# Linear attention and a cosine FFN in one planned program: copies of reciprocals on another engine, fewer weight tiles on GpSimd, other due dates

## Chip, cores and metric

One core of a Trainium2 chip runs the whole program. Its engines each take their own instructions strictly in order: TensorE (PE, with PEld for the weight load ahead of a matmul), VectorE (DVE), ScalarE (ACT), GpSimd (POOL) and SyncE (SP), which here only issues DMAs. The metric is device time in microseconds (us), the median over the runs of a kernel; lower is better.

## What is computed

Attention with an exponential feature map, without a softmax over keys, and behind it a feed-forward layer with the activation h cos(h). Sizes: batch 8, 8 heads, 576 positions, head width 64, 128 features; 4608 tokens, model width 512, inner width 2048, all in fp32.

```python
def phi(x):
    proj = np.einsum('bhsd,df->bhsf', x, w_phi)
    proj = proj - np.max(np.abs(proj), axis=-1, keepdims=True)
    return np.concatenate([np.exp(proj), np.exp(-proj)], axis=-1)
q_p, k_p = (phi(q), phi(k))
kv = np.einsum('bhsf,bhsd->bhfd', k_p, v)
z = np.sum(k_p, axis=2)
num = np.einsum('bhsf,bhfd->bhsd', q_p, kv)
den = np.einsum('bhsf,bhf->bhs', q_p, z)[..., None] + 1e-06
x = (num / den).transpose(0, 2, 1, 3).reshape(B * S, H * D)
h = x @ w_in
out = (h * np.cos(h)) @ w_out
```

## The kernel before, in words

**Attention.** The work is cut into 32 units, u0 to u31; a unit is two heads of one batch, so four units make a batch. Each unit runs one chain of steps: `load` and `load_v` (SP); `q_mm` (PE, L383), `q_copy` out of PSUM (ACT, L390), `q_red`, `q_max` and `q_turn` (DVE, L394, L402 and L404, L408), which bring the largest magnitude of each query position to all partitions; `q_sub` (POOL, L412); `k_mm` (PE, L437 and L440) and `k_max` (DVE, L447 and L449); `exp_k` and `exp_q` (ACT, L456 and L461); `kv_mm` (PE, L496 and L502) and `kv_out` (ACT, L510 and L511); `z_mm` (PE, L527) for the denominators, `invert` (DVE, L540 to L543) for their reciprocals; `spread` (POOL, L550), which copies the 9 reciprocals of each of 32 partitions to where the next step wants them, eight copies of 32x9 a unit; `turn` (DVE, L554), `n_mm` (PE, L535) for the numerators, `times` (DVE, L558), and `store`.

**FFN.** Tokens are cut into 9 chunks of 512, c0 to c8, and the inner width into 16 weight tiles, f0 to f15. A chunk and a weight tile give one FFN tile, 144 in all: `mm1` (PE, 12 matmuls, L641), `copy` out of PSUM (ACT, L647 and L648), `reduce` of the angle (DVE, L652), `cosine` (ACT, L656), `times` (DVE, L659), `high` (ACT, L48) and `low` (DVE, L53), `mm2` (PE, 12 matmuls, L675 to L677), which adds into four PSUM banks. Each operand is split into a high and a low part, so each product takes three matmuls. Before its first use each weight tile is unpacked and split (`convert`): `scale` and `high` on ACT, `bits` on DVE (L307, L309, L311), and three operations of 128x1024, `rest`, `low`, `add` (L318, L53, L324), on POOL for f0 to f7 and on DVE for f8 to f15.

**Stages.** Units u0 to u15 run at the start, together with the conversion of the weight tiles and the first visits of c0, c1 and c2; then FFN tiles of c0 to c2 run alone; then units u16 to u31 run beside c3 to c5, one unit to about three FFN tiles; at the end c6 to c8 run alone.

**Order.** Nothing is scheduled while the kernel runs. Every step is a `Step` with an engine, a cost, what it depends on, the buffers of a ring that it takes, and a due time. `plan()` (L81) walks forward in its own time: of the steps of an engine that could start within 0.05 us of the earliest, it takes the one with the least due time. On ACT a step that needs another function table counts as due 8 us later. A step with `port=True` also waits for, and holds, one shared resource: the SBUF way that DVE and POOL share. PSUM has 8 banks, and past the due time `FFN_DUE` attention steps may hold at most `A_BANKS` of them. The result is one fixed instruction order per engine.

ACT has to load a function table (ACT_TABLE_LOAD) when it goes from exponentials to the sine of `cosine` or back.

Of the kernel before, what the change touches and what calls it, by code (L numbers as in the profile page):

```python
# [17 lines left out]
P = 128  # L18
# [7 lines left out]
def phi_attention_then_cos_ffn(ctx: ExitStack, tc: tile.TileContext, qT, kT, vS, vT, w_phi, w_in, w_out, out):  # L26
# [40 lines left out]
    class Step:  # L67
        def __init__(self, eng, cost, fn, deps=(), take=(), use=(), due=0.0, lat=None, table=None, port=False):
            self.eng, self.cost, self.fn, self.due, self.table = eng, cost, fn, due, table
            self.deps = [d for d in deps if d is not None]  # L70
            self.take, self.use = list(take), list(use)
            self.port = port
            self.lat = LATENCY[eng] if lat is None else lat
            self.start = None
            for b in self.take + self.use:
                b.users.append(self)
            steps.append(self)

    LATENCY = dict(PE=0.35, ACT=0.25, DVE=0.2, POOL=0.25, SP=2.2)

    def plan():  # L81
# [15 lines left out]
        table = None  # L97
# [129 lines left out]
    A_BANKS = 5  # L227
    FFN_DUE = 60.0
    W_POOL = range(8)
# [24 lines left out]
    for v, (c, fts) in enumerate(course):  # L254
# [3 lines left out]
        for ft in fts:  # L258
            if ft not in seen:
                seen.add(ft)  # L260
                date_w[ft] = advance(0, W_DVE)[0]
            date_tile[n] = advance(T_PE, T_DVE)
            n += 1
            if v > 8 and len(date_unit) < NU and n % 3 == 0:
                date_unit[len(date_unit)] = advance(U_PE, U_DVE)
        at["DVE"] = max(at["DVE"], at["PE"] - 15)

    def due_unit(u, f):

        return date_unit[u][0] + f * max(date_unit[u][1], 20.0) - (0 if u < NBT else 16.0)  # L270
# [12 lines left out]
    def convert(ft):  # L283

        d = {}
        due = date_w[ft] - 14.0
# [56 lines left out]
    def reload(ft, after, due):  # L343
# [6 lines left out]
        w_ready[ft] = [Step("SP", 3.2, load, w_stored[ft] + [after], take=[slot], due=due)]  # L350
# [5 lines left out]
    stored, quotient = {}, {}  # L356

    def attention(u):
        d = {}
        early = u < EARLY  # L360
        due = lambda f: due_unit(u, f)
# [13 lines left out]
        ld = Step("SP", 1.9, load, take=[b["kr"], b["qr"]], due=due(-1.5))  # L375
        lv = Step("SP", 0.9, load_v, take=[b["v"]], due=due(-0.9))
# [33 lines left out]
        def q_sub(j):  # L410
            c = slice(j * S, (j + 1) * S)
            POOL.tensor_tensor(out=d["pq"][:, c], in0=d["pq"][:, c], in1=d["bq"][:, c], op=ALU.subtract)  # L412

        reds, mm = [], None
        for hf in range(2):
# [3 lines left out]
                      use=[b["qr"]] + ([b["pq"]] if hf else []), due=due(0.0))  # L419
            for j in range(2):  # L420
                cp = Step("ACT", 0.31, lambda hf=hf, j=j: q_copy(hf, j), [mm] + reds[:1], use=[pair[j], b["pq"]],
                          due=due(0.05))
                reds.append(cp)
        cps, reds = reds, []
        for i, cp in enumerate(cps):
            reds.append(Step("DVE", 0.42, lambda i=i: q_red(i // 2, i % 2), [cp], use=[b["pq"]], due=due(0.1)))
        qm = Step("DVE", 0.94, q_max, reds, take=[b["bq"]], use=[b["pq"]], due=due(0.15))
        qm = Step("DVE", 1.4, q_turn, [qm], use=[b["bq"]], due=due(0.16))
        qs = [Step("POOL", 1.5, lambda j=j: q_sub(j), [qm], use=[b["pq"], b["bq"]], due=due(0.2), port=True) for j in range(2)]


# [32 lines left out]
        for i in range(3):  # L464
            ps = d["kb", i] = Buf("bank", "a")
            pk = Buf("pk" if i < 2 else "pk_t")
            mm = Step("PE", 0.9 if i < 2 else 0.35, lambda i=i: k_mm(i), [ld], take=[ps, pk], use=[b["kr"]], due=due(0.12))
            kms.append(Step("DVE", 1.3 if i < 2 else 0.55, lambda i=i: k_max(i), [mm], use=[ps, pk], due=due(0.2)))
# [46 lines left out]
        for i in range(3):  # L515
            last = Step("PE", 1.15 if i < 2 else 0.5, lambda i=i: kv_mm(i), [lv, last] + (eks[i:i + 1] if early else eks),
                        take=[] if i else [acc, b["kv"]], use=[ekb[i], b["v"]] + ([acc, b["kv"]] if i else []), due=due(0.55))
        ko = Step("ACT", 0.6, kv_out, [last], use=[acc, b["kv"]], due=due(0.6))
# [19 lines left out]
        def invert():  # L538
# [4 lines left out]
            DVE.reciprocal(out=dn, in_=dn)  # L543

        def spread():
            d["d1"] = new("rb", [P, 2 * NJ], F32, f"d1_u{u}_", "d1")
            for g in range(4):
                for a in range(2):
                    r = 64 * (g // 2) + 32 * a
                    POOL.tensor_copy(out=d["d1"][r:r + 32, (g % 2) * NJ:(g % 2 + 1) * NJ], in_=d["dn"][32 * g:32 * g + 32])  # L550
# [14 lines left out]
        mm = Step("PE", 1.1, z_mm, [ko] + eqs, take=[zps], use=[b["kv"]] + eqb, due=due(0.72))  # L565
        dv = Step("DVE", 0.85, invert, [mm], take=[b["rb"]], use=[zps], due=due(0.8))
        dv = Step("POOL", 1.9, spread, [dv], use=[b["rb"]], due=due(0.8), port=True)
        dv = Step("DVE", 0.78, turn, [dv], use=[b["rb"]], due=due(0.81))
        outs = []
        for hf in range(2):  # L570
            ps = d["nb", hf] = Buf("bank", "a")
            mm = Step("PE", 1.05, lambda hf=hf: n_mm(hf), [mm], take=[ps], use=[b["kv"]] + eqb, due=due(0.75))
            outs.append(Step("DVE", 0.45, lambda hf=hf: times(hf), [mm, dv], use=[ps, b["rb"]], due=due(0.82)))
        stored[u] = Step("SP", 0.9, store, outs, use=[b["rb"]], due=due(0.9))
# [11 lines left out]
    def visit(v):  # L586
        c, fts = course[v]
        d = {}
        n0 = sum(len(x[1]) for x in course[:v])
# [5 lines left out]
        for kt in range(KT):  # L595
# [12 lines left out]
            chain["x"] = [Step("SP", 0.9, load, [stored[NHP * bt + kt] for bt in batches] + chain["x"], take=[raw], due=due_tile(n0, -2))]  # L608
            loads += chain["x"]
        for kt in range(KT):  # L610
# [11 lines left out]
            h = Step("ACT", 0.53, high, loads[kt] if v == 0 else [loads[kt]], take=[x], use=[rawb[kt]], due=due_tile(n0, -1))  # L622
            ks.append(Step("DVE", 0.68, low, [h], use=[x, rawb[kt]], due=due_tile(n0, -1), port=True))
# [4 lines left out]
        for i, ft in enumerate(fts):  # L628
# [53 lines left out]
            s1 = Step("PE", 2.75, mm1, ks + w_ready[ft] + chain["mm1"], take=[ps, hs], use=xb + [slot], due=due_tile(n, 0.0))  # L682
            chain["mm1"] = [s1]
            s2 = Step("ACT", 1.18, copy, [s1], take=[g], use=[ps, hs], due=due_tile(n, 0.3))
            s3 = Step("DVE", 0.74, reduce, [s2], use=[g, hs], due=due_tile(n, 0.4), port=True)
            s4 = Step("ACT", 0.62, cosine, [s3], use=[g], due=due_tile(n, 0.6), table="s")
            s5 = Step("DVE", 0.66, times, [s4], use=[g, hs], due=due_tile(n, 0.8), port=True)
# [93 lines left out]
```

## Time and profile before

| what | value |
|---|---|
| median of 3 runs | 1213.09 us (1210.26 to 1213.25) |
| the profiled execution | 1212.26 us |
| its span, first to last instruction | 1210.5 us |
| instructions | 19112 |
| mean granted TensorE clock | 0.98 |
| POOL busy | 225.5 us, 358 instructions |
| DMA | 160.77 MB, mean 133 GB/s |

The span is the window in which the profile sees instructions; the 1.8 us beside it are start and end of the execution. Busy times of an engine are sums over its instructions. Names such as `pq_u__7912` are tiles: `u` stands for a unit, `c` for a chunk, `f` for a weight tile, and the number tells one buffer from another. `bank` is PSUM.

### The profile page before, as it was taken

The page shows a single profiled execution, that of the slowest core. Times are in us where ns is not written, and L with a number is a line of the kernel's source. Part 1 is how long each engine was busy: PE and PEld are TensorE (multiplying, and loading weights), DVE is VectorE, ACT ScalarE, POOL GpSimd, SP SyncE. Part 2 cuts the span into 40 slices and gives each one's busy share as a digit, 9 for nine tenths or more (in the row PEclk, how much of TensorE's full clock was granted, in tenths as well). Part 3 has the DMA queues.
Part 4 walks back from the last instruction along what each step waited for, and adds up shares of the span by engine and source line. Part 5 has one row for each costly group of instructions (what it writes and reads, how often), then busy time and mean ns, then how long its engine had stood idle before and what let it go on. Part 6 is the DMA issues. An engine that isn't in the chain of part 4 may idle for free.

```text
span 1210.5 us, 19112 instructions
## 1 busy us (share of the span) xinstructions
PE 1142.1 (94%) x7360; PEld 849.1 (70%) x7360; DVE 774.7 (64%) x1310; ACT 700.3 (58%) x1262; POOL 225.5 (19%) x358
## 2 busy tenths in 40 slices
PE   7776989899999999999998999999999999999997
PEld 5544646568668888767675766677677788888886
DVE  6999797997879755456666565675555534433432
ACT  6555758678666554556556555584666645544442
POOL 2556554620110000011111111121111100000000
PEclk9988989999999999999998999999999999999999
DMA  5444552743664523354212542236510360250350
GB/s 172 141 166 145 188 186 104 226 136 122 232 186 174 191 87 108 127 204 140 86 50 84 184 145 98 59 102 216 174 29 11 132 221 23 105 179 30 120 193 36
DMA packets 92764, 160.77 MB, mean 133 GB/s; under 512 B 43776, under 2 KB 52224, under 8 KB 84480
## 3 DMA queue, kind: packets, MB, share of 16 engines
q1 hardware_dynamic: 92672, 159.54, 39.5%
q8 instruction: 58, 0.95, 0.3%
q14 instruction: 34, 0.28, 0.1%
HBM read 117.57 MB, written 41.94 MB: 132 GB/s over the span
## 4 chain that ended last, share of the span: by engine, by line
PE 69%; ACT 11%; DVE 6%; DMA 3%; issue 1%; POOL 0%; SPq 0%; DVEq 0%; ACTq 0%
PE bank L641 27%; PE bank L675 10%; PE bank L676 9%; PE bank L677 9%; PE bank L535 3%; PE bank L437 3%; PE bank L496 3%; PE bank L527 2%; PE bank L383 1%; ACT L456 1%; ACT L656 1%; PE bank L502 1%; PE bank L440 0%; DVE m_u__1467 L404 0%; DVE o L717 0%
## 5 line engine op out<-in xcount | busy, mean ns | idle before, releaser
L656 ACT ACT_TABLE_LOAD x24 | 30.8, 1283 | 0.4
L550 POOL COPY d_u__4884<-dn_u__4879 32x9 f32<-32x9 f32 x8 | 2.2, 275 | 150.8 <-DVE dn_u__4879 L543 150.5
L456 ACT ACT_TABLE_LOAD x21 | 26.9, 1283 | 2.3 <-DVE pk_u__6191 L449 2.0
L717 DVE COPY o<-bank 128x512 f32<-128x512 f32 x18 | 12.1, 682 | 13.5 <-PE bank L677 10.5
L715 ACT ACTIVATE o<-bank 128x512 f32<-128x512 f32 x18 | 10.6, 597 | 12.9 <-PE bank L677 10.7
L711 DVE TENSOR_TENSOR o<-bank,o 128x512 f32<-128x512 f32 x24 | 15.5, 682 | 0.3
L641 PE MATMUL bank<-xh_c__5003,w 128*128 128x512 f32 x32 | 13.7, 429 | 0.0
L641 PE MATMUL bank<-xh_c__4449,w 128*128 128x512 f32 x32 | 13.5, 421 | 0.0
L641 PE MATMUL bank<-xh_c__6056,w 128*128 128x512 f32 x32 | 13.4, 418 | 0.0
L641 PE MATMUL bank<-xh_c__7275,w 128*128 128x512 f32 x32 | 12.7, 396 | 0.0
L641 PE MATMUL bank<-xh_c__5512,w 128*128 128x512 f32 x32 | 12.6, 393 | 0.0
L641 PE MATMUL bank<-xh_c__4491,w 128*128 128x512 f32 x32 | 12.6, 393 | 0.0
L641 PE MATMUL bank<-xh_c__6530,w 128*128 128x512 f32 x32 | 12.6, 393 | 0.0
L641 PE MATMUL bank<-xh_c__5325,w 128*128 128x512 f32 x32 | 12.5, 392 | 0.0
L641 PE MATMUL bank<-xh_c__4454,w 128*128 128x512 f32 x32 | 12.5, 392 | 0.0
L641 PE MATMUL bank<-xh_c__5774,w 128*128 128x512 f32 x32 | 12.5, 392 | 0.0
L641 PE MATMUL bank<-xh_c__6341,w 128*128 128x512 f32 x32 | 12.5, 391 | 0.0
L641 PE MATMUL bank<-xh_c__4537,w 128*128 128x512 f32 x32 | 12.5, 391 | 0.0
L641 PE MATMUL bank<-xh_c__6802,w 128*128 128x512 f32 x32 | 12.5, 391 | 0.0
L641 PE MATMUL bank<-xh_c__7477,w 128*128 128x512 f32 x32 | 12.5, 390 | 0.0
L641 PE MATMUL bank<-xh_c__7820,w 128*128 128x512 f32 x32 | 12.5, 390 | 0.0
L641 PE MATMUL bank<-xh_c__7674,w 128*128 128x512 f32 x32 | 12.5, 390 | 0.0
(3810 smaller groups left out, 4250.0 us busy)
## 6 DMA issues: line engine op xcount, KB each, us to landing
w<-w_parts SPq DMA_DIRECT2D x48, 1024.0 KB, 4.8
w_parts<-w SPq DMA_DIRECT2D x16, 1024.0 KB, 4.8
out<-o SPq DMA_DIRECT2D x36, 256.0 KB, 2.1
vmain<-vS SPq DMA_DIRECT2D x32, 256.0 KB, 3.9
sums<-o SPq DMA_DIRECT2D x24, 256.0 KB, 2.2
o<-sums SPq DMA_DIRECT2D x24, 256.0 KB, 3.0
vtail<-vT SPq DMA_DIRECT2D x64, 16.0 KB, 2.8
w_raw_f__139<-w_in SPq DMA_DIRECT2D x1, 512.0 KB, 4.2
```

The source lines that it names most:

```text
L383: PE.matmul(out=ps[j], lhsT=wphi[r, :], rhs=d["qr"][r, hf * HALF:(hf + 1) * HALF], start=True, stop=True)
L437: PE.matmul(out=ps[:, 256 * x:256 * x + 256], lhsT=d["kr"][:, P * s:P * s + P], rhs=wk_f, start=(x == 0), stop=True, skip_group_check=True)
L456: ACT.activation(out=e[:, :, s * P:(s + 1) * P], in_=pk, func=AF.Exp, scale=1.0 - 2.0 * s)
L496: PE.matmul(out=acc[c:c + 64, n, j, :], lhsT=e[:, 2 * x + j, P * n + c:P * n + c + 64], rhs=vmain[u % 2][:, s, j, :], start=(s == 0 and j ...
L527: PE.matmul(out=ps[32 * g:32 * g + 32], lhsT=d["z"][:, 2 * n + j, :], rhs=d["eq", j][:, n, hf * HALF:(hf + 1) * HALF], start=(n == 0), sto ...
L535: PE.matmul(out=ps[64 * j:64 * j + 64], lhsT=d["kv"][:, 2 * n + j, :], rhs=d["eq", j][:, n, t], start=(n == 0), stop=(n == 1))
L641: PE.matmul(out=h, lhsT=a[:, cs], rhs=d[b, kt], start=(k == 0), stop=(k == 3 * KT - 1))
L656: ACT.activation(out=m["g"], in_=m["g"], func=AF.Sin, bias=halfpi, scale=1.0)
L675: PE.matmul(out=a, lhsT=gh[:, t], rhs=w[:, 0], start=first, stop=False)
L676: PE.matmul(out=a, lhsT=gh[:, t], rhs=w[:, 1], start=False, stop=False)
L677: PE.matmul(out=a, lhsT=gl[:, t], rhs=w[:, 0], start=False, stop=last)
L711: DVE.tensor_tensor(out=o, in0=bank(acc[tb]), in1=o, op=ALU.add)
```

## The change

Five things change; what is computed stays.

1. `invert` writes the reciprocals straight into the wider tile `d1`, in both of its halves (128x18 instead of 128x9), and `spread` is four ACT copies of 32x9, each between partition groups that are neighbours, instead of eight POOL copies.
2. POOL takes `rest`, `low` and `add` of f0 to f3 alone; those of f4 to f7 go to DVE.
3. The planner counts `q_max` and `invert` as users of the way that DVE and POOL share, too, and charges 0.1 us when PE goes between FFN and attention matmuls.
4. `A_BANKS` is 6 instead of 5, and the `load_v` of a unit comes behind that of the unit before.
5. Every kind of step has a shift of its due time (`EARLIER`, in us, by kind and stage). The names `SPAN`, `SHIFT`, `EVERY`, `LEAD`, `TURN` and `SLACK` hold the values that stood in the code before.

```diff
-        def __init__(self, eng, cost, fn, deps=(), take=(), use=(), due=0.0, lat=None, table=None, port=False):
-            self.eng, self.cost, self.fn, self.due, self.table = eng, cost, fn, due, table
+        def __init__(self, eng, cost, fn, deps=(), take=(), use=(), due=0.0, lat=None, table=None, port=False, kind=""):
+            self.eng, self.cost, self.fn, self.table = eng, cost, fn, table
...
+            self.kind, self.due = kind, due + EARLIER.get(kind, 0.0)
...
+            if eng == "PE":
+                self.table = "x" if fn.__name__ in ("mm1", "mm2", "one") else "f"
...
+    EARLIER = {
+        "a.exp_k": 3, "a.exp_q": 17, "a.invert": -86, "a.k_mm": 27, "a.kv_mm": 3, "a.kv_out": 40, "a.load": 4,
...
-            if x.eng == "ACT" and x.table is not None and x.table != table:
-                c += 1.3
-                table = x.table
+            if x.table not in (None, table.get(x.eng)):
+                c += 1.3 if x.eng == "ACT" else 0.1
+                table[x.eng] = x.table
...
-    A_BANKS = 5
+    A_BANKS = 6
...
-    W_POOL = range(8)
+    W_POOL = range(4)
...
-        lv = Step("SP", 0.9, load_v, take=[b["v"]], due=due(-0.9))
+        lv = Step("SP", 0.9, load_v, [chain_v.get(u - 1)], take=[b["v"]], due=due(-0.9), kind=phase + "load_v")
...
-        qm = Step("DVE", 0.94, q_max, reds, take=[b["bq"]], use=[b["pq"]], due=due(0.15))
+        qm = Step("DVE", 0.94, q_max, reds, take=[b["bq"]], use=[b["pq"]], due=due(0.15), port=True, kind=phase + "q_max")
...
-            DVE.reciprocal(out=dn, in_=dn)
+            d1 = d["d1"] = new("rb", [P, 2 * NJ], F32, f"d1_u{u}_", "d1")
+            DVE.reciprocal(out=d1.rearrange("p (h b) -> p h b", h=2), in_=dn.unsqueeze(1).broadcast_to([P, 2, NJ]))
 
         def spread():
-            d["d1"] = new("rb", [P, 2 * NJ], F32, f"d1_u{u}_", "d1")
-            for g in range(4):
-                for a in range(2):
-                    r = 64 * (g // 2) + 32 * a
-                    POOL.tensor_copy(out=d["d1"][r:r + 32, (g % 2) * NJ:(g % 2 + 1) * NJ], in_=d["dn"][32 * g:32 * g + 32])
+
+            for q in range(4):
+                c = slice((1 - q % 2) * NJ, (2 - q % 2) * NJ)
+                r, o = 32 * q, 32 * (q ^ 1)
+                ACT.activation(out=d["d1"][r:r + 32, c], in_=d["d1"][o:o + 32, c], func=AF.Copy, scale=1.0)
...
-        dv = Step("DVE", 0.85, invert, [mm], take=[b["rb"]], use=[zps], due=due(0.8))
-        dv = Step("POOL", 1.9, spread, [dv], use=[b["rb"]], due=due(0.8), port=True)
+        dv = Step("DVE", 0.9, invert, [mm], take=[b["rb"]], use=[zps], due=due(0.8), port=True, kind=phase + "invert")
+        dv = Step("ACT", 0.9, spread, [dv], use=[b["rb"]], due=due(0.8), kind=phase + "spread")
```

What this does to the order is seen at three places. The first is POOL in the early stage, from the second half of f3's conversion on. `pq` is what `q_sub` works on, `w_t` and `w` belong to a weight tile, and `d1` is written by `spread`. Before:

```order
L53 TENSOR_TENSOR w_t1_f3__961<-w_t1_f3__961,w_985 128x1024
L550 COPY d1_u4__1061<-dn_u4__1008 32x9 x8
L324 TENSOR_TENSOR w_985<-w_t1_f3__961,w_t2_f3__962 128x1024
L412 TENSOR_TENSOR pq_u6__1000<-pq_u6__1000,bq_u6__1047 128x576 x2
L318 TENSOR_TENSOR w_t2_f4__1131<-w_t2_f4__1131,w_t0_f4__1129 128x1024
L53 TENSOR_TENSOR w_t1_f4__1130<-w_t1_f4__1130,w_1178 128x1024
L550 COPY d1_u5__1246<-dn_u5__1223 32x9 x8
L324 TENSOR_TENSOR w_1178<-w_t1_f4__1130,w_t2_f4__1131 128x1024
L550 COPY d1_u6__1395<-dn_u6__1383 32x9 x8
L412 TENSOR_TENSOR pq_u7__1260<-pq_u7__1260,bq_u7__1391 128x576 x2
```

And POOL in the changed kernel, from the same tile on:

```order
L442 TENSOR_TENSOR pq_u6__931<-pq_u6__931,bq_u6__1013 128x576 x2
L53 TENSOR_TENSOR w_t1_f3__998<-w_t1_f3__998,w_1062 128x1024
L344 TENSOR_TENSOR w_t2_f3__999<-w_t2_f3__999,w_t0_f3__997 128x1024
L350 TENSOR_TENSOR w_1062<-w_t1_f3__998,w_t2_f3__999 128x1024
L442 TENSOR_TENSOR pq_u7__1156<-pq_u7__1156,bq_u7__1293 128x576 x2
L442 TENSOR_TENSOR pq_u8__1316<-pq_u8__1316,bq_u8__1417 128x576 x2
L442 TENSOR_TENSOR pq_u9__1498<-pq_u9__1498,bq_u9__1590 128x576 x2
L442 TENSOR_TENSOR pq_u10__1660<-pq_u10__1660,bq_u10__1759 128x576 x2
```

From u7 on POOL has nothing but `q_sub` left. On DVE, up to the last product (`times`) of u12, the changed order holds eight of the operations of 128x1024 that POOL had, and the `bits` of two weight tiles fewer (seven tiles' instead of nine).

The second place is ACT in the late stage, around the exponentials of u25: `g` and `hs` are written by `copy` (L647 and L648 before, L679 and L680 now), `ek` and `eq` by the exponentials. Before:

```order
L647 ACTIVATE g_c4__7054<-bank3_72 128x512
L648 ACTIVATE hs_c4__7053<-bank3_72 128x512
L456 ACT_TABLE_LOAD
L456 ACTIVATE ek_u25__7071<-pk_u25__6916 128x4x128 x2
L456 ACTIVATE ek_u25__7087<-pk_u25__6963 128x4x128 x2
L456 ACTIVATE ek_u25__7090<-pk_u25__6967 128x128 x2
L461 ACTIVATE eq_u25__7093<-pq_u25__6892 128x576 x2
L461 ACTIVATE eq_u25__7112<-pq_u25__6892 128x576 x2
L656 ACT_TABLE_LOAD
L656 ACTIVATE g_c4__7054<-g_c4__7054,halfpi_81 128x512
L390 ACTIVATE pq_u26__7137<-bank2_71 128x288
```

The same place in the changed kernel, from the reciprocals' copies of u24 (L581) on:

```order
L581 ACTIVATE d1_u24__6885<-d1_u24__6885 32x9 x4
L679 ACTIVATE g_c4__6927<-bank0_69 128x512
L680 ACTIVATE hs_c4__6926<-bank0_69 128x512
L486 ACT_TABLE_LOAD
L486 ACTIVATE ek_u25__6971<-pk_u25__6940 128x4x128 x2
L486 ACTIVATE ek_u25__6986<-pk_u25__6962 128x4x128 x2
L486 ACTIVATE ek_u25__7001<-pk_u25__6966 128x128 x2
L679 ACTIVATE g_c4__7005<-bank1_70 128x512
L680 ACTIVATE hs_c4__7004<-bank1_70 128x512
L491 ACTIVATE eq_u25__7008<-pq_u25__6594 128x576 x2
L491 ACTIVATE eq_u25__7028<-pq_u25__6594 128x576 x2
L688 ACT_TABLE_LOAD
```

The block of exponentials now has the `copy` of an FFN tile in its middle, and the copies of reciprocals stand ahead of the `copy` in front of it. Behind the second table load stand the cosines of both tiles. Over the whole program ACT has 52 table loads instead of 48; the four more are in the early stage.

The third place is PE at the same time. Before, behind the last matmul of a `mm2`, the `kv_mm` of u25 runs in one piece, and the `k_mm` of u26 (into banks 2 and 5) comes right after it:

```order
L677 MATMUL bank6_75<-w_6451,gl_c4__7057 128x512
L496 MATMUL bank3_72<-vmain1_88,ek_u25__7071 64x65 x16
L496 MATMUL bank3_72<-vmain1_88,ek_u25__7087 64x65 x16
L502 MATMUL bank3_72<-vtail1_90,ek_u25__7090 64x130 x4
L437 MATMUL bank2_71<-wk_f_83,kr_u26__6760 128x256 x2
L437 MATMUL bank5_74<-wk_f_83,kr_u26__6760 128x256 x2
L527 MATMUL bank3_72<-eq_u25__7093,z_u25__7151 32x288
```

In the changed kernel the second piece of that `kv_mm` is followed by the `q_mm` (L413) of u27, and then by a `mm2` (L707 and on):

```order
L526 MATMUL bank4_73<-vmain1_88,ek_u25__6986 64x65 x16
L413 MATMUL bank5_74<-qr_u27__6956,wphi_78 128x288
L413 MATMUL bank1_70<-qr_u27__6956,wphi_78 128x288
L532 MATMUL bank4_73<-vtail1_90,ek_u25__7001 64x130 x4
L707 MATMUL bank7_76<-w_6460,gh_c4__6876 128x512
```

Between the first and the second piece of `kv_mm` stands the `mm1` of a further FFN tile, and the `k_mm` of u26 comes only after `n_mm` of u25. In this stretch a `mm2` comes three `mm1` after the `mm1` of its own tile, where it was one or two before.

More of the change, by code (lines that the diff above doesn't have):

```diff
@@ L77, in __init__ @@
             steps.append(self)
+    EARLIER = {
+        "a.exp_k": 3, "a.exp_q": 17, "a.invert": -86, "a.k_mm": 27, "a.kv_mm": 3, "a.kv_out": 40, "a.load": 4,
+        "a.load_v": 30, "a.n_mm": 16, "a.q_copy": -4, "a.q_max": -9, "a.q_mm": -8, "a.q_sub": 2, "a.q_turn": -45,
+        "a.spread": -2, "a.store": -2, "a.times": -8, "a.turn": 27, "a.z_mm": -8, "b.invert": 1, "b.k_max": 5,
+        "b.k_mm": 12, "b.kv_mm": 5, "b.kv_out": -4, "b.load": 33, "b.n_mm": -26, "b.q_copy": -42, "b.q_max": 4,
+        "b.q_mm": -3, "b.q_red": 4, "b.q_turn": 3, "b.spread": -8, "b.store": -29, "b.turn": 22, "b.z_mm": -12,
+        "c.exp_k": -68, "c.exp_q": -10, "c.invert": 8, "c.k_max": -5, "c.k_mm": 9, "c.kv_out": -50, "c.load": -14,
+        "c.load_v": -33, "c.n_mm": -21, "c.q_copy": 1, "c.q_max": -52, "c.q_mm": -24, "c.q_red": -33, "c.q_sub": -13,
+        "c.spread": 17, "c.turn": -41, "c.z_mm": -30, "m.copy": 4, "m.fetch": -1, "m.load": 32, "m.low": -22,
+        "m.mm1": 14, "m.mm2": 2, "m.one": -2, "m.out_copy": -19, "m.out_store": -34, "m.reduce": 13, "m.times": 15,
+        "m.x_high": -6, "m.x_low": -16, "n.copy": -33, "n.cosine": 7, "n.high": 104, "n.load": 26, "n.low": -8,
+        "n.mm2": 16, "n.out_copy": 36, "n.out_store": -45, "n.reduce": -7, "n.x_low": 2, "r.load": -69, "w.add": 60,
+        "w.bits": 4, "w.high": -22, "w.load": -20, "w.low": -4, "w.rest": 34, "w.scale": -12,
+    }
+    TURN = dict(ACT=8.0, PE=0.0)
+    SLACK = dict(PE=0.05, ACT=0.05, DVE=0.05, POOL=0.05, SP=0.05)
     LATENCY = dict(PE=0.35, ACT=0.25, DVE=0.2, POOL=0.25, SP=2.2)
@@ L681, in visit @@
             slot = w_slot[ft]
-            s1 = Step("PE", 2.75, mm1, ks + w_ready[ft] + chain["mm1"], take=[ps, hs], use=xb + [slot], due=due_tile(n, 0.0))
+            s1 = Step("PE", 2.75, mm1, ks + w_ready[ft] + chain["mm1"], take=[ps, hs], use=xb + [slot], due=due_tile(n, 0.0), kind=stage + "mm1")
             chain["mm1"] = [s1]
-            s2 = Step("ACT", 1.18, copy, [s1], take=[g], use=[ps, hs], due=due_tile(n, 0.3))
-            s3 = Step("DVE", 0.74, reduce, [s2], use=[g, hs], due=due_tile(n, 0.4), port=True)
@@ L686, in visit @@
-            s4 = Step("ACT", 0.62, cosine, [s3], use=[g], due=due_tile(n, 0.6), table="s")
-            s5 = Step("DVE", 0.66, times, [s4], use=[g, hs], due=due_tile(n, 0.8), port=True)
-            s6 = Step("ACT", 0.53, high, [s5], take=[gh], use=[g], due=due_tile(n, 1.0))
-            s7 = Step("DVE", 0.68, low, [s6], take=[gl], use=[g, gh], due=due_tile(n, 1.2), port=True)
+            s2 = Step("ACT", 1.18, copy, [s1], take=[g], use=[ps, hs], due=due_tile(n, 0.3), kind=stage + "copy")
+            s3 = Step("DVE", 0.74, reduce, [s2], use=[g, hs], due=due_tile(n, 0.4), port=True, kind=stage + "reduce")
```

103 lines of the change are left out of this document (60 added, 43 removed).

## The prediction, made before the changed kernel was run

> **What bounds the kernel now.** I read the page first: which engine is busy, and in which slices it is not.
>
> ```profile
> PE 1142.1 (94%) x7360; PEld 849.1 (70%) x7360; DVE 774.7 (64%) x1310; ACT 700.3 (58%) x1262; POOL 225.5 (19%) x358
> PE   7776989899999999999998999999999999999997
> DVE  6999797997879755456666565675555534433432
> PEclk9988989999999999999998999999999999999999
> PE 69%; ACT 11%; DVE 6%; DMA 3%; issue 1%; POOL 0%; SPq 0%; DVEq 0%; ACTq 0%
> ```
>
> PE is the bound on the whole, but its first eight slices are not full, and there DVE is the fuller engine. So I asked for busy times by stage, cut at 242.6 (`z_mm` of u12), 349.3 (of u15), 513.9 (of u16) and 947.3 (of u31).
>
> ```profile
> 8.00:242.60 234.60, 196.57 (x1778) 127.12 (x1777) 211.20 (x358) 153.10 (x297) 124.30 (x146) 0.93 0.52 167
> 242.60:349.30 106.70, 103.17 (x675) 76.53 (x674) 88.74 (x141) 79.63 (x135) 16.08 (x30) 1.00 0.54 178
> 349.30:513.90 164.60, 164.60 (x803) 133.51 (x802) 109.88 (x166) 92.53 (x156) 5.74 (x10) 1.00 0.40 134
> 513.90:947.30 433.40, 419.08 (x2959) 300.39 (x2958) 260.94 (x489) 257.37 (x479) 74.83 (x150) 0.99 0.34 111
> 947.30:1210.50 263.20, 257.07 (x1149) 210.61 (x1148) 103.96 (x159) 116.12 (x196) 3.34 (x8) 0.99 0.33 118
> ```
>
> Columns: length; busy us of PE, PEld, DVE, ACT, POOL; granted clock; DMA share; GB/s. In the **early stage** PE idles 234.6 - 196.6 = 38 us and has a clock of 0.93, while DVE is busy for 90%: DVE is the bound. In the **late stage** PE idles 433.4 - 419.1 = 14.3 us and DVE and ACT have room. The second and third stage and the last (but for some 6 us at its end) are full on PE: nothing that the change does to other engines can gain there, and what the two other stages gain is kept to the end. So at most 38 + 14 us of visible idle time, and what the clock gives, are to be had.
>
> **Early stage: four weight tiles leave POOL.** What POOL does to DVE is seen in the timeline around f5's conversion, POOL first.
>
> ```profile
> 150.97 2.37 POOL L318 TENSOR_TENSOR w_t_f__1313<-w_t_f__1313,w_t_f__1311 128x1024 f32<-128x1024 f32 x1
> 153.30 2.35 POOL L53 TENSOR_TENSOR w_t_f__1312<-w_t_f__1312,w 128x1024 f32<-128x1024 f32 x1
> 155.73 2.41 POOL L324 TENSOR_TENSOR w<-w_t_f__1312,w_t_f__1313 128x1024 fp32r<-128x1024 f32 x1
> ...
> 152.67 0.72 DVE L402 TENSOR_TENSOR m_u__1466<-m_u__1416 64x36 f32<-64x36 f32 x1
> 153.42 4.99 DVE L404 TENSOR_TENSOR m_u__1467<-m_u__1466 32x36 f32<-32x36 f32 x4
> ```
>
> The same two lines elsewhere, from the source lines' rows:
>
> ```profile
> L402 DVE TENSOR_TENSOR m_u__178<-m_u__136 x1: 191/191/191, 14.4 to 14.4; 64x36 f32<-64x36 f32 x1
> L404 DVE TENSOR_TENSOR m_u__179<-m_u__178 x4: 184/186/189, 14.7 to 15.3; 32x36 f32<-32x36 f32 x4
> ```
>
> So four instructions of 0.19 us took 4.99 us: DVE was held for (0.72 - 0.19) + (4.99 - 0.75) = 4.8 us, twice until a POOL operation ended. For f6 and f7 the chain of waits shows the like, behind their own `add` on POOL; the last two rows give a free operation of the first kind and the DVE price of one of the moved operations.
>
> ```profile
> 190.27 2.88 DVE g_c__1824 L659
> 224.99 2.48 DVE m_u__2227 L404
> 884.39 0.69 DVE L659 TENSOR_TENSOR g_c__8078<-hs_c__8077,g_c__8078 128x512 f32<-128x512 f32 x1 [7.54 <-ACT g_c__8078 L656]
> L318 DVE TENSOR_TENSOR w_t_f__2312<-w_t_f__2312,w_t_f__2310 x1: 1217/1217/1217, 259.3 to 259.3; 128x1024 f32<-128x1024 f32 x1
> ```
>
> f6 held DVE for 2.88 - 0.69 = 2.2 us, f7 for 2.48 - 0.19 = 2.3 us, f5 for 4.8: a mean of 3.1, so four tiles 12 to 13 us. Bounds: nothing, if POOL met an idle DVE, and all three operations, 4 x (2.37 + 2.35 + 2.41) = 28.5 us. I take **-13**. Against it DVE must do these operations itself. Up to `times` of u12 the new order puts eight of them there, 8 x 1.217 = 9.7 us, and leaves out two tiles' `bits`:
>
> ```profile
> 97.48 0.60 DVE w_t_f__960 L307
> 98.18 1.24 DVE w_t_f__961 L309
> 99.44 0.69 DVE w_t_f__960 L311
> ```
>
> That is 2 x 2.5 = 5.1 us less, so **+4.7**. The four remaining operations and the two `bits` run after 242.6, where DVE has 18 and 55 us of room beside a full PE: nothing. Without that cover they would cost 10 us.
>
> **Early stage: the copies of reciprocals.**
>
> ```profile
> L550 POOL COPY d_u__366<-dn_u__316 x8: 181/184/189, 27.4 to 29.0; 32x9 f32<-32x9 f32 x8
> L550 POOL COPY d_u__1772<-dn_u__1725 x8: 188/380/1221, 176.9 to 180.9; 32x9 f32<-32x9 f32 x8
> L511 ACT ACTIVATE z_u__274<-bank x1: 273/273/273, 21.2 to 21.2; 128x128 f32<-128x128 f32 x1
> L543 DVE RECIPROCAL dn_u__316<-dn_u__316 x1: 216/216/216, 26.1 to 26.1; 128x9 f32<-128x9 f32 x1
> ```
>
> Eight POOL copies last 1.8 us undisturbed and up to 5.2 us. An ACT copy of 32x9 is in no row: between nothing and the 0.27 us of 128x128, and I take 0.2, near POOL's 0.18 for the same shape. Four are then 0.8 us (0 to 1.1), one microsecond less on the way from `invert` to `turn`. The doubled reciprocal costs 0 to 0.2 us; I take 0. That way is rarely the last wait of PE: of 13 units I count two, **-2** (0 to -13). [...] ACT pays 32 x 0.8 = 26 us, 10 of it in a stage where it is busy 153 of 234 us, and four table loads, 5 us by the row of 1.28 us below: hidden as long as nobody waits behind them, otherwise up to +5.
>
> **Early stage: the shared way counted for `q_max`.** The rows of L402 and L404 above are what an uncounted collision costs. The planner now keeps them apart from `q_sub`, too, whose pair lasts 3 us. I take one avoided collision of 2 us, **-2**; 0 to -8, a quarter to all of four. Six banks instead of five, `load_v` in order and 0.1 us for PE's turns set the order alone: nothing by themselves. **Early: -13 + 4.7 - 2 - 2 = -12**, from +5 to about -30.
>
> **Late stage.** Here I looked for what PE waits for in a regular period, in the timeline and the chain of waits.
>
> ```profile
> 870.54 3.26 POOL L412 TENSOR_TENSOR pq_u__7912<-pq_u__7912,bq_u__8050 128x576 f32<-128x576 f32 x2 [7.27 <-DVE bq_u__8050 L408]
> 870.71 1.81 DVE L652 SCALAR_TENSOR_TENSOR g_c__8047<-g_c__8047,hs_c__8046 128x512 f32<-128x512 int32 x1 [0.34 <-ACT hs_c__8046 L648]
> 876.14 1.28 ACT L456 ACT_TABLE_LOAD   x1
> 882.34 1.28 ACT L656 ACT_TABLE_LOAD   x1
> 884.71 2.11 PE L437 MATMUL bank<-wk_f,kr_u__7776 128*128 128x256 f32 x8 [0.94 <-ACT pq_u__8161 L390]
> ...
> 857.01 2.10 PE bank L437 x8
> 912.39 2.10 PE bank L437 x8
> 643.35 4.43 DMA xs<-rb_u__5981
> 647.83 3.06 DMA x_raw_c__6029<-xs
> ```
>
> `k_mm` recurs after 27.7 us and each time stands 0.94 us: its bank is freed by a `q_copy` that ACT does only after the whole block of exponentials and two table loads, and the block itself began late because `reduce`, `cosine` and `times` of one FFN tile ran ahead of it, `reduce` held by POOL (1.81 us instead of 0.69). In the new order the block is broken by a `copy`, `q_mm` of the unit after next gives PE work early, and each `mm2` is three tiles behind its `mm1`, so no FFN tile's chain stands on PE's way. ACT's work a period is far below 27 us (257 us over 15 periods), so PE should run without this gap. Nine such periods give back 8 us; the irregular ones, where ACT stood before an x load after 643, give 2 of the remaining 6. **-10**, from +2 (two more turns a unit between attention and FFN on PE, about 0.1 us each) to -15.
>
> **Sum.** 1212.26 (the profiled execution, 1.8 us over its span, 0.8 under the median of 1213.09) - 12 - 10 = 1190.3; beside the median 1191. I say **1190**.
>
> **Rivals.**
>
> *DVE is not relieved.* The moved operations cost DVE as much as the collisions did, since POOL's often met an idle DVE; early 0, late -10: 1202. For it: DVE is 90% busy and gets work. Against it: three of the four tiles show 2.2 to 4.8 us. Chance 0.17.
>
> *The late loop stays.* Another wait in ACT's queue replaces the old one and PE keeps its 0.94 us: 1200. Chance 0.08.
>
> *The spread blocks ACT (slower).* The four copies wait for `invert` on DVE, and behind them in ACT's queue stand the `copy` that frees the bank for PE's `k_mm`, the table load and all exponentials. After `z_mm` PE has `q_mm`, `n_mm` and `mm1` before that `copy` could start, about 0.7 + 1.1 + 2.9 by these rows of the chain:
>
> ```profile
> 893.53 0.69 PE bank L383 x4
> 888.34 1.12 PE bank L535 x8
> 921.91 2.97 PE bank L641 x12
> ```
>
> That is 4.7 us, against 0.9 for `invert`, 0.8 for the copies and some 0.3 for signals. It decides from a DVE that is 2.7 us late; one hold by POOL is 1 to 2.3 us, so it takes two, or a queue. If each late unit then lost 1.3 us: 16 x 1.3 = +21, half the early gain, 1227. Chance 0.13.
>
> *PE stays warm.* Early PE runs at 0.93 of its clock, 16 us in 234.6. If the pauses that cost the clock go, the stage gains up to half of its 38 us of idle time and half of those 16, -27, and the late one -14: 1171. [...] Chance 0.10.
>
> *Nothing that can be measured*: gains and new waits cancel, 1212. Chance 0.05.
>
> **How the numbers follow.** The forecast holds 0.47, with 1180 to 1198 as its own range. With the rivals, 1168 to 1213 leaves out most of the slow case (0.13) and a tail of the fast one. A measurement of this kernel can tell about 0.3% from no change. Faster: 0.47 + 0.17 + 0.08 + 0.10 = 0.82; same 0.05; slower 0.13.
>
> **What would show it.** Right: `times` of u12 some 12 us earlier, no DVE row of L402 and L404 over 1 us after f3, `k_mm` of the late units without idle time before it, PE idle under 5 us in that stage. Wrong: in the waits, ACT standing before the `d1` copies, or PE before `kv_mm` or `z_mm` each period; DVE busy in the early stage no less, at the same length.

## The result, and the profile after

| | before | after |
|---|---|---|
| median | 1213.09 us (1210.26 to 1213.25) | 1165.52 us (1165.31 to 1165.83) |
| ratio, with its 95% interval | | 0.9613 (0.9597 to 0.9630) |
| profiled execution, its span | 1212.26, 1210.5 | 1165.31, 1163.5 us |

The change takes 47.6 us off, twice the 23 that were forecast, and the time lies below the range. From the page of the changed kernel come the busy times, two engines' slices, the clock, and the shares of the chain that ended last:

```profile
PE 1130.5 (97%) x7360; PEld 841.7 (72%) x7360; DVE 753.2 (65%) x1322; ACT 735.0 (63%) x1394; POOL 127.8 (11%) x90
PE   7879999899999999999999999999999999999998
DVE  6999998987899946466656655566655434433333
PEclk9989999999999999999999999999999999999999
PE 87%; ACT 2%; DVE 1%; DMA 1%; issue 0%; SPq 0%; DVEq 0%
```

POOL has lost 98 us and ACT has gained 35, as the moves say. But PE's share of the chain rose from 69% to 87%: what was taken away is time in which PE waited. Where, the stages tell. They are cut at the same work as before (`z_mm` of u12, u15, u16, u31), with the same columns (length; busy us of PE, PEld, DVE, ACT, POOL; granted clock; DMA share; GB/s):

```profile
8.00:216.00 208.00, 188.87 (x1776) 121.63 (x1774) 193.48 (x362) 159.99 (x339) 69.87 (x38) 0.96 0.54 172
216.00:325.10 109.10, 107.35 (x694) 77.93 (x696) 92.58 (x143) 86.36 (x151) 9.59 (x6) 1.00 0.53 180
325.10:498.40 173.30, 173.30 (x843) 139.56 (x843) 125.03 (x190) 104.78 (x181) 7.22 (x4) 1.00 0.45 154
498.40:898.60 400.20, 400.20 (x2899) 289.08 (x2898) 237.69 (x472) 264.58 (x523) 39.91 (x28) 1.00 0.35 116
898.60:1163.50 264.90, 259.78 (x1161) 212.94 (x1160) 104.37 (x157) 118.02 (x201) 0.00 (x0) 1.00 0.34 118
```

**Early stage**: 234.6 us became 208.0, with eight FFN tiles in both: 26.6 less, where 12 were forecast. PE's idle time went from 38 us to 208.0 - 188.9 = 19.1, the clock from 0.93 to 0.96. **Late stage**: 433.4 became 400.2, and PE is busy for all of it. This is not yet the gain, since the stretch now holds 45 FFN tiles instead of 47. A tile is 24 matmuls that begin 0.227 us apart in the trace, 5.44 us, so two are 10.9, and like for like the stage lost about 22 us, where 10 were forecast. The rest went to the neighbours: the two middle stages are 11 us longer, with one and a half tiles more.

What the early stage gained is seen in PE's waits there. Before, from 8 to 242.6 us (who waits, for whom; us in all, times, longest):

```profile
PE bank L527 <- ACT z_u__1559 L511: 5.4, 1, 5.4
PE bank L496 <- ACT eq_u__1100 L461: 4.7, 1, 4.7
PE bank L437 <- DMA kr_u__765<-kT: 4.0, 1, 4.0
PE bank L641 <- POOL w L324: 3.7, 1, 3.7
PE bank L496 <- ACT ek_u__595 L456: 3.7, 2, 3.5
```

And after, from 8 to 216 us:

```profile
PE bank L413 <- DVE rb_u__680 L589: 3.2, 1, 3.2
PE bank L557 <- ACT z_u__937 L541: 3.1, 1, 3.1
PE bank L673 <- DVE xl_c__819 L53: 2.7, 1, 2.7
```

Before, PE stood five times for 3.5 us or longer, 21.3 us in all: three times for ACT, once for a load, once for POOL. After, no wait is longer than 3.2, and two of the three longest are for DVE.

A row names only the last step ahead of PE. Followed back along the chain of work, the second row of before (4.7) leads to two DVE operations that POOL holds, which last 0.69 us each when they are free. The sixth row is for DVE itself, behind the hold of f7 at 224.99:

```profile
100.73 2.78 DVE g_c__933 L659
103.52 2.79 DVE g_c__976 L652
PE bank L383 <- DVE rb_u__2251 L558: 3.0, 1, 3.0
```

The longest row (5.4) has no DVE in it: ahead of this `kv_out` in ACT's queue stands the `scale` of a weight tile, which could begin only at 157.45, after 3.2 us of waiting for its load. So DVE, the fullest engine there, stands behind some of PE's waits and not behind others.

In the late stage of before the waits are

```profile
PE bank L496 <- ACT o L715: 5.0, 1, 5.0
PE bank L496 <- ACT pq_u__5046 L390: 3.0, 1, 3.0
PE bank L437 <- ACT pq_u__7137 L390: 0.9, 1, 0.9
```

and further ones of 0.8 and 0.9 at L437; after, the same view has no row at all.

**What a wait costs beyond its length** shows at the first of these rows. The `kv_mm` piece behind the wait of 5.0 us, in the timeline of before (start, duration; in brackets the idle time ahead of it):

```profile
659.80 2.00 PE L496 MATMUL bank<-vmain,ek_u__6075 128*64 128x65 f32 x32 [4.96 <-ACT o L715]
```

and a piece of the same shape without a wait, in the changed kernel:

```profile
700.47 1.16 PE L526 MATMUL bank<-vmain,ek_u__6721 128*64 128x65 f32 x32
```

The granted clock is 0.50 from 657.95 to 664.70, and the piece behind the wait lasts 2.00 us instead of 1.16: this wait cost more than its length. I therefore count as lost in a stage PE's idle time and half of the time that PE was busy at half the clock, both summed over the trace's records; the half is an estimate (the `mm1` matmuls behind one of the long pauses below begin 0.43 us apart at first, 0.23 later). The tables below use this sum. Before, it is 38.0 + 27.1 / 2 = 51.6 us early, 3.5 in the middle, 14.3 + 8.4 / 2 = 18.5 late. After, it is 19.1 + 15.9 / 2 = 27.1, 1.7 and 0. The sums differ by 73.6 - 28.8 = 44.8 us, and the spans by 47.0: nearly all of the gain is waits of PE and the clock that they cost. What made PE wait is a further question.

### The profile page after: what moved, and what is told of

Read it like the earlier page. It is cut to its first block, busy times and chain, and to the rows that moved or that the text cites. A ratio compares the mean times of both kernels' runs of the same rounds, so it can differ in the third digit from the quotient of the medians.

```text
span 1163.5 us, 19048 instructions
## 1 busy us (share of the span) xinstructions
PE 1130.5 (97%) x7360; PEld 841.7 (72%) x7360; DVE 753.2 (65%) x1322; ACT 735.0 (63%) x1394; POOL 127.8 (11%) x90
## 4 chain that ended last, share of the span: by engine, by line
PE 87%; ACT 2%; DVE 1%; DMA 1%; issue 0%; SPq 0%; DVEq 0%
PE bank L673 33%; PE bank L707 12%; PE bank L709 11%; PE bank L708 11%; PE bank L565 5%; PE bank L526 4%; PE bank L467 4%; PE bank L413 3%; PE bank L557 2%; PE bank L532 1%; PE bank L470 0%; ACT L688 0%; DMA x_raw_c__1547<-xs 0%; DMA x_raw_c__2388<-xs 0%; DVE w_t_f__998 L335 0%
## 5 line engine op out<-in xcount | busy, mean ns | idle before, releaser
L673 PE MATMUL bank<-xh_c__6064,w 128*128 128x512 f32 x32 | 13.5, 423 | 0.0
L673 PE MATMUL bank<-xh_c__5095,w 128*128 128x512 f32 x32 | 13.5, 423 | 0.0
L442 POOL TENSOR_TENSOR pq_u__3431<-pq_u__3431,bq_u__3829 128x576 f32<-128x576 f32 x2 | 4.1, 2086 | 79.4 <-ACT w_t_f__3825 L329 79.4
```

The source lines that it names most:

```text
L673: PE.matmul(out=h, lhsT=a[:, cs], rhs=d[b, kt], start=(k == 0), stop=(k == 3 * KT - 1))
```

## The experiments

Two theories stood against each other; the expectations call them B and A. **Engines** (B): the moves from POOL to DVE and ACT relieve the fullest engine (the forecast's early term). **Order** (A): the engines on which the moved operations run don't matter; the new order, which the due times and the planner's rules make, keeps PE from waiting.

### The same order on other engines

In the changed kernel the planner still plans `spread` as an ACT step and f4 to f7 as DVE's, so all dates and orders stay, but the code issues them where they were before:

```diff
+        if ft < 8:
+            eng = POOL
...
-            DVE.reciprocal(out=d1.rearrange("p (h b) -> p h b", h=2), in_=dn.unsqueeze(1).broadcast_to([P, 2, NJ]))
+            DVE.reciprocal(out=dn, in_=dn)
...
-                ACT.activation(out=d["d1"][r:r + 32, c], in_=d["d1"][o:o + 32, c], func=AF.Copy, scale=1.0)
+                    POOL.tensor_copy(out=d["d1"][r:r + 32, (g % 2) * NJ:(g % 2 + 1) * NJ], in_=d["dn"][32 * g:32 * g + 32])
```

> The changed kernel's order is kept on every engine, but the copies of reciprocals go back to eight POOL copies (with the narrow reciprocal), and the three large operations of f4 to f7 back to POOL. If the order gives the gain (theory A), this stays near the changed kernel: 1168 to 1182 us, DVE held a few us more by POOL in the early stage. If the relief of POOL and DVE gives it (theory B), most of the gain is lost: 1190 to 1210 us.

Measured: 1165.5 us, ratio 0.9605 (0.9587 to 0.9624), the whole gain without any of the moves, just below the expected range. Its early stage:

```profile
8.00:217.60 209.60, 187.68 (x1772) 120.69 (x1770) 186.19 (x354) 149.40 (x291) 114.78 (x142) 0.98 0.53 171
```

Read DVE's column: 186.2 us with the old engines, 193.5 with the new ones. The eight operations that DVE took over cost it 9.7 us and made it 7.3 us busier, so they spared it only some 2 or 3 us of being held. It is still held at `q_max`, twice behind f3, the second time just after the early stage (L434 is the first line of it in this kernel; free it takes 0.19 us):

```profile
L434 DVE TENSOR_TENSOR m_u__1288<-m_u__1175 x1: 1689/1689/1689, 120.5 to 120.5; 64x36 f32<-64x36 f32 x1
L434 DVE TENSOR_TENSOR m_u__2522<-m_u__2453 x1: 2229/2229/2229, 225.1 to 225.1; 64x36 f32<-64x36 f32 x1
```

PE's idle time there is 21.9 us instead of 19.1 and its time at half the clock 9.7 instead of 15.9: 26.8 us lost against 27.1. So holding DVE for these few us cost nothing here.

The counterpart: the order of before, with four ACT copies and f4 to f7 on DVE.

```diff
+        if 4 <= ft < 8:
+            eng = DVE
...
-                    POOL.tensor_copy(out=d["d1"][r:r + 32, (g % 2) * NJ:(g % 2 + 1) * NJ], in_=d["dn"][32 * g:32 * g + 32])
+                ACT.activation(out=d["d1"][r:r + 32, c], in_=d["d1"][o:o + 32, c], func=AF.Copy, scale=1.0)
```

> The order of before is kept, but the copies of reciprocals are four ACT copies and the large operations of f4 to f7 run on DVE, each at the place that it had in the program. Theory A: little, 1203 to 1216 us. Theory B: most of the gain, 1175 to 1195 us.

Measured: 1217.24 us, ratio 1.0039 (1.0023 to 1.0055): no gain, slightly slower. Early, DVE is busy for 213.2 us instead of 211.2, so the holds that went were about as much as the work that came, and PE's long waits stay; the longest, for the same `kv_out` of ACT, is longer. In the timeline ACT stands 3.47 us ahead of it for the `add` of f5, which is now DVE's:

```profile
8.00:248.00 240.00, 199.25 (x1780) 128.26 (x1778) 213.20 (x374) 163.94 (x345) 73.11 (x38) 0.91 0.52 166
...
PE bank L529 <- ACT z_u__1531 L513: 7.1, 1, 7.1
PE bank L498 <- DVE pk_u__1055 L451: 4.3, 1, 4.3
PE bank L439 <- DMA kr_u__754<-kT: 3.9, 1, 3.9
```

So the moves do not carry the gain in either order. A third step in this direction puts the operations of f0 to f3 on DVE as well, in the new order (`eng = DVE` for every weight tile):

> The changed kernel's order, with the large operations of f0 to f3 on DVE as well, so that POOL has only the subtractions. With f4 to f7 the engine made no difference, so 1163 to 1168 us; if the four first tiles on POOL still hold DVE on PE's way: 1152 to 1160 us.

Measured: 1169.76 us, ratio 0.9645 (0.9617 to 0.9672), 4 us worse than the changed kernel and outside both expected ranges: PE idles 24.5 us early. Freeing POOL further does not help.

Whether DVE's holds matter is not the same question as whether the moves do, for the order can keep DVE and POOL apart as well. I sum the holds over the trace's records: what a DVE operation lasts beyond the lower quartile of the times of its line and shape, where that is more than 0.25 us. Beside each such operation POOL is busy for at least that long. Early stage, us:

| kernel | length | DVE busy | held by POOL | PE's loss |
|---|---|---|---|---|
| before | 234.6 | 211.2 | 43.0 | 51.6 |
| old order, new engines | 240.0 | 213.2 | 29.5 | 55.2 |
| new order, old engines | 209.6 | 186.2 | 22.3 | 26.8 |
| changed | 208.0 | 193.5 | 20.8 | 27.1 |
| new order, all weight tiles on DVE | 215.5 | 197.5 | 11.0 | 32.7 |
| changed, all due-time shifts at zero (below) | 221.0 | 205.3 | 23.5 | 38.6 |

On the old engines the order alone takes away 20.7 us of holds; DVE is busy for 25.0 us less, and the stage is 25.0 us shorter. So part of what the order gains may come by way of DVE, and these runs do not separate that from its other effects on PE's waits. Fewer holds are not enough, though. In the old order the moves take away 13.5 us of them and bring as much work in their place, and nothing is gained. The last row has nearly the holds of the changed kernel and loses 11.5 us more. And in the new order DVE is 7.3 us busier on the new engines, at no cost: there it is not the bound.

### What makes the order

The kernel before with the table `EARLIER` and nothing else of the change; and the changed kernel without the table:

```diff
-            self.eng, self.cost, self.fn, self.due, self.table = eng, cost, fn, due, table
+            self.kind, self.due = kind, due + EARLIER.get(kind, 0.0)
```

```diff
-            self.kind, self.due = kind, due + EARLIER.get(kind, 0.0)
+            self.kind, self.due = kind, due
```

> The kernel of before with the table of due dates alone; engines, banks and the planner's rules are the old ones. Theory A in its strong form (the dates alone do it): 1170 to 1185 us. If the dates fit only the planner and the engines that they were found with: anything from 1190 to 1230 us.

> The changed kernel with all shifts of due dates at zero: engines, banks and the planner's rules are the new ones. Theory A: the gain is gone, 1200 to 1220 us. Theory B: most of it stays, 1175 to 1190 us.

Measured: 1177.64 us, ratio 0.9706 (0.9689 to 0.9724), with the dates alone, and 1185.7 us, 0.9772 (0.9755 to 0.9788), without them. The second lies in the range that went with the theory of the engines, though the two swaps above show that the engines do not carry it; the order changes without the dates, too. The dates alone give 2.9%, the rest alone 2.3%, both together 3.9%: each brings part of the same gain. Which of the other parts it is, three runs on the kernel before tell, without dates: `A_BANKS = 6`; `port=True` on `q_max` and `invert`; the moves to ACT and DVE, planned as such.

```diff
-    A_BANKS = 5
+    A_BANKS = 6
```

> The kernel of before with A_BANKS 6 instead of 5, nothing else; no dates. Without dates the changed kernel is 27 us faster than before, and three rules can carry that. If the banks do (attention steps may hold one bank more, so PE has more to choose from): 1185 to 1200 us. If not: 1205 to 1220 us.

```diff
-        qm = Step("DVE", 0.94, q_max, reds, take=[b["bq"]], use=[b["pq"]], due=due(0.15))
+        qm = Step("DVE", 0.94, q_max, reds, take=[b["bq"]], use=[b["pq"]], due=due(0.15), port=True)
-        dv = Step("DVE", 0.85, invert, [mm], take=[b["rb"]], use=[zps], due=due(0.8))
+        dv = Step("DVE", 0.85, invert, [mm], take=[b["rb"]], use=[zps], due=due(0.8), port=True)
```

> The kernel of before, with q_max and invert counted by the planner as users of the way that DVE and POOL share, nothing else. If this rule carries the 27 us: 1185 to 1200 us, with less idle time of PE in the early and in the late stage. If not: 1205 to 1220 us.

```diff
-    W_POOL = range(8)
+    W_POOL = range(4)
...
-        dv = Step("POOL", 1.9, spread, [dv], use=[b["rb"]], due=due(0.8), port=True)
+        dv = Step("ACT", 0.9, spread, [dv], use=[b["rb"]], due=due(0.8))
```

> The kernel of before with the copies of reciprocals on ACT and the large operations of f4 to f7 on DVE, and the planner told of it (its costs too), so that the order changes with them; five banks, ports as before, no dates. Put into the old order these moves gave nothing (1217 us). If the planner needs them to find the better order: 1185 to 1200 us; if they do nothing in the plan either: 1205 to 1220 us.

Measured: the banks 1216.33 us, 1.0030 (1.0007 to 1.0053); the counting of the shared way 1197.21, 0.9886 (0.9858 to 0.9915); the moves 1207.36, 0.9951 (0.9922 to 0.9979). So the moves, which are worth nothing in a fixed order, give about half a per cent when the planner may arrange its order around them (with executions from 1201.6 to 1210.9 us), and the rule on the shared way gives 1.1%. The charge for PE's turns and the order of `load_v` have no run of their own. Dates and the rule on the shared way together, on the old engines:

> The kernel of before with the due dates and with q_max and invert counted on the shared way; old engines, costs and banks. If dates and this rule make the order together: 1163 to 1170 us. If the dates fit only the whole set of rules and costs that they stand beside: 1172 to 1190 us.

Measured: 1179.91 us, 0.9740 (0.9712 to 0.9768), not better than the dates alone. The 12 us from the dates alone to the changed kernel come with neither the rule nor, in a fixed order, the moves. They need something else of the rest: the sixth bank, the charge, the order of `load_v`, or the new engines and costs in the plan. None of these was run beside the dates, so which it is stays open.

Then groups of the dates were taken out of the changed kernel: those of the late units and their FFN tiles (`c.` and `n.`), all but those, those of the early units (`a.` and `b.`), and those of the early FFN tiles and weights (`m.`, `w.`, `r.`). The edit for the first is this; the others differ in the letters:

```diff
-            self.kind, self.due = kind, due + EARLIER.get(kind, 0.0)
+            self.kind, self.due = kind, due + (EARLIER.get(kind, 0.0) if kind[:1] in "abmwr" else 0.0)
```

> The changed kernel without the shifts of due dates for the late units and the FFN visits after the first nine; the early ones stay. If each stage's gain comes from its own dates: the early stage keeps its 27 us of lost PE time, the late one has again the 7 us of the kernel without dates, 1172 to 1178 us. If the late stage gets its order from the rules: 1165 to 1169 us.

> The changed kernel with the due dates of the late units and the later FFN visits alone; those of the early stage are zero. If the gains of the stages add up: the early stage loses some 41 us of PE again (27 with its dates), the late one nothing, 1176 to 1181 us. If the late dates do not fit a late stage that begins differently: above 1182 us.

> The changed kernel without the due dates of units u0 to u15; those of early FFN tiles, weights and of the late stage stay. If the units' dates make the early gain: early loss near 41 us, 1176 to 1185 us. If those of FFN tiles and weights do: near 27 us, 1164 to 1170 us.

> The changed kernel without the due dates of the weights and of the first nine FFN visits; those of the units and of the late stage stay. If the units' dates make the early gain: 1164 to 1172 us. If the FFN's and weights' dates do: 1176 to 1185 us.

Times and ratios as measured; the us lost as above, by stage:

| dates left out | us | ratio | lost early | lost late |
|---|---|---|---|---|
| none | 1165.52 | 0.9613 (0.9597 to 0.9630) | 27.1 | 0 |
| late | 1177.91 | 0.9727 (0.9691 to 0.9763) | 27.0 | 9.1 |
| early | 1176.77 | 0.9714 (0.9684 to 0.9745) | 39.0 | 0 |
| units, early | 1179.27 | 0.9735 (0.9704 to 0.9766) | 42.4 | 0 |
| FFN and weights, early | 1175.68 | 0.9705 (0.9677 to 0.9733) | 39.7 | 0 |
| all | 1185.70 | 0.9772 (0.9755 to 0.9788) | 38.6 | 6.7 |

Each stage has its dates: the late ones bring about 12 us and leave the early loss as it is, the early ones bring about 11 us and leave the late stage full. Within the early stage the parts are not additive: leaving out either half of its dates costs as much as leaving out all. Without the late dates the regular gap is back, as PE's waits from 479 to 908 us say:

```profile
PE bank L526 <- issue: 3.1, 2, 1.6
PE bank L467 <- ACT pq_u__6786 L420: 1.5, 1, 1.5
PE bank L467 <- ACT pq_u__8045 L420: 0.9, 1, 0.9
PE bank L467 <- ACT pq_u__8282 L420: 0.9, 1, 0.9
```

From the second row on this is `k_mm` behind a `q_copy`, the wait that the forecast's late term was about.

### What a pause costs

PE is full in the last stage of the changed kernel, so pauses can be put there and measured by themselves. Ahead of ten `mm1` of c7 and ten of c8 stands a chain from PE over ACT and POOL back to PE, with one POOL copy or with six; the added matmuls write into a bank that `mm1` then begins anew.

```diff
+                if c >= 7 and 2 <= i < 12:
+                    PE.matmul(out=h[:, 0:P], lhsT=wk_f[:, 0:P], rhs=wk_f[:, 0:P], start=True, stop=True)
+                    ACT.activation(out=gap_a, in_=h[:, 0:32], func=AF.Copy, scale=1.0)
+                    for _ in range(6):
+                        POOL.tensor_copy(out=gap_b.rearrange("p (n e) -> p n e", e=32), in_=gap_a.unsqueeze(1).broadcast_to([P, 16, 32]))
+                    PE.matmul(out=h[:, 0:P], lhsT=gap_b[:, 0:P], rhs=wk_f[:, 0:P], start=True, stop=True)
```

> The changed kernel with twenty pauses put on PE in its last stage (chunks c7 and c8), where it has none: a small matmul, an ACT copy of it, one POOL copy, and a second small matmul that reads that, ahead of the first product of a tile; what these write is not used. Pauses of about 1.5 us. If lost time is the idle time plus half of the time at half clock, and short pauses leave the clock alone: slower by the 20 pauses and the 40 small matmuls, 30 to 45 us, granted clock 1.00 there.

> The same with six POOL copies in each pause, some 4 us of it. If a pause of that length brings the clock down: each costs its length and about 1.7 us more, the granted clock of the stage falls to about 0.8, and the time beyond the idle sum is 30 us or more. If the clock does not matter: slower by the idle sum and the small matmuls alone, as with the short pauses.

Measured: 1202.12 us, ratio 0.9913 (0.9885 to 0.9942), with one copy; 1325.34 us, 1.0922 (1.0895 to 1.0948), with six. The last stage and PE's waits in it, short pauses:

```profile
898.60:1200.00 301.40, 275.13 (x1244) 223.62 (x1242) 105.48 (x157) 121.47 (x221) 13.14 (x20) 1.00 0.30 103
...
PE bank L675 <- POOL gap_b L674: 21.4, 20, 1.5
```

Long pauses:

```profile
898.60:1320.00 421.40, 321.50 (x1245) 258.26 (x1243) 108.25 (x157) 121.50 (x221) 81.50 (x120) 0.85 0.21 74
...
PE bank L675 <- POOL gap_b L674: 96.2, 20, 5.5
```

The stage had 264.9 us. Short pauses make it 36.5 longer: 21.4 of waiting and 15.1 for the 40 added matmuls, at a clock of 1.00. Long ones make it 156.5 longer: 96.2 of waiting, the same 15.1, and 45.2 more, at a clock of 0.85. So here a pause of about 1.0 us costs its length, and one of 4.8 us costs 2.3 us on top, where the estimate was 1.7. The timeline behind one long pause shows that price (start, duration):

```profile
992.87 0.80 PE L675 MATMUL bank<-wk_f,gap_b 128*128 128x128 f32 x2 [4.69 <-POOL gap_b L674]
993.32 0.77 PE L681 MATMUL bank<-xh_c__8375,w 128*128 128x512 f32 x1
993.89 0.63 PE L681 MATMUL bank<-xh_c__8382,w 128*128 128x512 f32 x1
994.32 0.63 PE L681 MATMUL bank<-xh_c__8510,w 128*128 128x512 f32 x1
...
996.02 0.39 PE L681 MATMUL bank<-xh_c__8510,w 128*128 128x512 f32 x1
996.25 0.40 PE L681 MATMUL bank<-xh_c__8690,w 128*128 128x512 f32 x1
```

`mm1`'s matmuls begin 0.43 us apart for some 2.7 us, then 0.23 us apart. Pauses longer than the short ones and shorter than the long ones were not put in; the last section has some that occurred.

No run beat the changed kernel; its order with the old engines ties with it.

## Why the prediction was wrong

**The early term failed as a mechanism.** The step is "DVE is busy for 90%: DVE is the bound", with the terms -13, +4.7, -2 and -2 worked out from it, so that what the moves take off DVE the stage gains. The prices were nearly right: an ACT copy of 32x9, taken at 0.2 us, lasts

```profile
L581 ACT ACTIVATE d_u__373<-d_u__373 x4: 208/209/211, 29.4 to 30.1; 32x9 f32<-32x9 f32 x4
```

In the old order the moves do take 13.5 us of holds off DVE, and in the changed kernel no `q_max` is held any more behind f3; the last such row (L434) is

```profile
L434 DVE TENSOR_TENSOR m_u__829<-m_u__828 x4: 184/188/2289, 76.4 to 79.2; 32x36 f32<-32x36 f32 x4
```

But the moves bought nothing: undone in the new order they leave the time as it is, and done in the old order they do not lower it. The relief that the forecast credited to them comes from the order: of the 43.0 us of holds it takes 20.7 on the old engines, and the moves 1.5 more. And DVE's busy share was no price of PE's waits: in the new order DVE is busy for 7.3 us more without any loss, and the longest wait of before stands behind a load in ACT's queue. The forecast had PE's waits in its hands and priced an engine's share instead.

**"Set the order alone: nothing by themselves" was the other half of that error.** It was said of the banks, `load_v` and PE's turns; the early dates got no term at all, and the rule on the shared way, -2, gives some 14 us alone, 6 of them in the early stage. On the old engines, the order alone shortens the early stage from 234.6 to 209.6 us: 25 of its 26.6. By the table, the rules and costs alone bring the early loss from 51.6 to 38.6 us, the early dates from there to 27.1.

**The late mechanism was right, its size was not.** The term was "k_mm without its 0.94 us", -10, of which 8 for nine regular gaps and 2 for the irregular waits. PE's waits show seven of these gaps, 6.3 us in all, and two irregular waits, 8.0 us in all. `k_mm` of the late units has no idle time before it any more, and all 14.3 us of idle time went, the irregular 5.0 and 3.0 too. The half clock behind those two (8.4 us at half rate, 4.2 lost) was left out of the sum, although the long wait and the slow `kv_mm` behind it stand in the trace of before. Idle time and clock make 18.5 of the 22; the rest is within the like-for-like correction for tiles.

**The rivals.** "DVE is not relieved" was right in what it says of DVE (2.0 us more in the old order, 7.3 in the new) and wrong in its time, 1202, since the order brings the early gain. "PE stays warm", 1171, came nearest: pauses that cost the clock went. Its size was half of 38 us idle and half of the clock's 16; measured are 18.9 of 38.0 idle and 5.6 of 13.6. "The spread blocks ACT" did not happen: PE waits for nothing in the late stage, and in the old order with the new engines that stage has 432.5 us against 433.4. "The late loop stays" and "nothing that can be measured" fell with the 400.2 of 400.2 us.

**What stays open.** How much of the early gain comes by way of DVE's holds; which single dates, or which rule beside the shared way, bring the last 12 us. Of the early loss 27.1 us are still there after the change.

## What to carry to other kernels

Where one engine is the bound and waits, list its own waits, longest first, follow each back along the chain, and price the change by which of them it takes away; a neighbour's busy share of 90% does not yet say that anyone waits for it. A change that reorders is tested by holding the order and swapping the engines, and by holding the engines and swapping the order. Shifts of due times are worth what the rules and costs beside them make of them: here the same shifts gave 12 us less on the old ones, and the gains of parts don't add up.

## What the runs showed of the hardware

The clock fell after pauses shorter than the 4.8 us of the experiment, too. In the late stage of before the wait of 3.0 us ends at 545.26, and the window behind it has the granted clock 0.50:

```profile
545.30:548.60 3.30, 3.30 (x35) 2.94 (x36) 3.13 (x9) 2.73 (x6) 0.00 (x0) 0.50 0.11 45
```

In the two kernels each of twelve pauses of 2.6 to 5.4 us (eight before, four after) is followed, at once or within 1.4 us, by a stretch at half the clock, and none of those between 1.3 and 1.8 us is. One stretch before, with a clock of 0.50 from 60.58 to 63.90 us, has no such pause ahead of it. Nor does the length alone tell the two kinds apart in another run: in the old order with the new engines a pause of 1.80 us ends at 322.30 and has half the clock behind it, and one of 3.02 us ends at 552.41 and has not:

```profile
322.50:325.70 3.20, 3.20 (x35) 2.34 (x34) 2.68 (x7) 0.83 (x3) 0.00 (x0) 0.50 0.75 264
552.50:556.00 3.50, 3.50 (x70) 2.95 (x71) 3.29 (x10) 2.68 (x6) 0.00 (x0) 1.00 0.10 42
```

No view of the profile shows what sets these two apart. In these runs the pauses that cost the clock and those that did not overlap between 1.8 and 3.0 us.
